# Full products for the first chunk, and the folds of two inputs moved to other quarters

## The chip, the cores and the metric

The kernel runs on one core of a Trainium2 chip. The metric is the time of one execution in microseconds of the device; a profiled execution also leaves a span, from its first to its last instruction. TensorE multiplies matrices and writes PSUM. VectorE, ScalarE and POOL (GpSimd) work on tiles, and SP only issues DMAs. In the profile they are PE (with PEld for its weight loads), DVE, ACT, POOL and SP.

## The reference

```python
batch, seq, dim = (8, 3008, 256)          # x, float32

X = np.fft.fft(x, axis=1)                 # over the sequence
X = np.fft.fft(X, axis=2)                 # over the features
x = X.real

xt = x.transpose(0, 2, 1)
h = np.maximum(xt @ w_tok1, 0.0) @ w_tok2         # 3008 -> 256 -> 3008
u = x + h.transpose(0, 2, 1)
h2 = np.maximum(u @ w_ch1, 0.0) @ w_ch2           # 256 -> 1536 -> 256
return u + h2
```

For each of eight batches this takes the real part of a two-dimensional Fourier transform, mixes along the sequence with a two-layer network, and then along the features with another one.

## The kernel before

All matmuls are in float16 with sums in float32. The work of one batch has three parts.

**The fold.** `fold(b)` (L451) takes the batch's input from `xp` and `xm` and uses the symmetries of the transform: it adds mirrored rows and mirrored columns into `eo`. It is a generator of 12 steps, three for each of four ranges of rows: L463 adds `xm` into `xp` (before the first, L461 and L462 treat column 0), L467 and L472 write the two halves of `eo`. All of them run on VectorE. `load_x(b)` (L157) fills `xp` with four DMAs and `xm` with two gathers, all issued by POOL. There is one buffer of `xp`, of `xm` and of `eo`, so the load of one input waits for the last fold step of the input before it.

**The front.** `front(b)` (L570) and `rest(b)` (L605) form a generator of the transform and the first network: `inner` and `outer` make `z` from `eo`, L596 to L601 make `w`, L613 and L636 the hidden layer `uu`, `third` makes a third of `yt` (L645 on TensorE, L648 on ScalarE, L652 on VectorE), and L730 with L738 make `ut`, the transposed input of the second network, in six chunks of 512 columns (the last has 448). `turn_u(b, c)` turns a chunk back by two DMA transposes on SP, into `rt`, which is needed for the residual.

**The second network.** For each chunk `(b, c)`, `mm1` (L765) makes 12 tiles of the hidden layer `c1` on TensorE (L773), which ScalarE brings out of PSUM with a ReLU (L776). `mm2` (L867) then multiplies with `wc2`. A chunk for which `plain(b, c)` is true takes full products: for each of four row blocks 12 matmuls with 256 columns, and residuals on VectorE. All other chunks take `mm2_sums` (L801), which gets the product of 2 x 2 blocks with seven block products instead of eight. It needs sums of blocks of `c1`, four instructions per half chunk on VectorE (`block_sums`, L790, into `sb` and in place into `c1`), and sums of blocks of `wc2` (`weight_sums`, L235). Its products go to the two PSUM tiles `px` and `py`, all of 128 columns; ScalarE keeps three of them as `m` (L822), VectorE and POOL add them into `osb` (L799), and SP writes `osb` out.

**The order.** It is written out by hand. The loop over `b` and over six chunks `c` has four quarters `s` for each chunk, so a batch has 24 quarters, `sub = 4 * c + s`, from 0. Each quarter issues three of the chunk's `mm1` tiles (six matmuls), and a quarter of `mm2` of the *previous* chunk; between them it takes steps of the generators as lists say:

- `own_plan[b][sub]`: steps of this batch's own front that are left (the `ut` of chunks 1 or 2 to 5);
- `plan[b][sub]`: steps of the next batch's front;
- `early_plan[sub]`: in batch 0, steps of `fold(1)`;
- `fold_plan[b][sub]`: steps of `fold(b + 2)`; in batch 1, of `fold(2)` to its end and then of `fold(3)`.

`load_x(2)` is issued in quarter 11 of batch 0 and `load_x(3)` in quarter 1 of batch 1, `load_x(1)` ahead of the loop. `block_sums` of a chunk run in its quarters 2 and 3 for one half and in the first two quarters of the next chunk for the other half. For chunk (0, 0) all of it runs in the next chunk, as instructions of twice the size. Every engine works off its instructions in the order in which they were issued: a VectorE instruction that waits for data holds all VectorE instructions behind it.

PSUM has three buffers for `pc` ("mm"), three for `pz`, `pw`, `pt`, `pq`, `py` of `third` and `pu` ("f"), and two for the products of `mm2` ("o2").

Of the kernel before, what the change touches and what calls it, by code (L numbers as in the profile page):

```python
# [21 lines left out]
BB = 8  # L22
# [12 lines left out]
NCH = 6  # L35
# [6 lines left out]
def kernel(  # L42
# [42 lines left out]
    def dram(t, offset, ap):  # L85
        return bass.AP(tensor=t, offset=offset, ap=ap)
# [65 lines left out]
    def gather(out_, rows, index):  # L152
        nc.gpsimd.indirect_dma_start(
            out=out_, out_offset=None, in_=rows,
            in_offset=bass.IndirectOffsetOnAxis(ap=index, axis=0))

    def load_x(b):  # L157
        xp = xin.tile([KR, NR, D], FP16, tag="xp", name="xp")
        xm = xin.tile([KG, NR - 1, D], FP16, tag="xm", name="xm")
        for i in range(2):  # L160
            for q, n in ((0, 32), (32, NQ - 32)):
                p0 = i * NQ + q
                nc.gpsimd.dma_start(
                    out=xp[p0:p0 + n, :, :],
                    in_=dram(x_t, (b * S + 16 * i + 64 * q) * D,
                             [[64 * D, n], [1, NR * D]]))
        xmf = xm[:].rearrange("p t d -> p (t d)")
        for k in range(2):
            gather(xmf[:, 8 * D * k:8 * D * (k + 1)], x8, ix8[0:KG, b, k:k + 1])
        return xp, xm  # L170
# [5 lines left out]
    x_tiles = {0: load_x(0)}  # L176
# [50 lines left out]
    HC = NCT // 2  # L227
# [216 lines left out]
    def align_w2(c, th, e):  # L444
        a = slice(8 * c, min(8 * c + 8, NQ))
        copy(e, w2p[:, th, :, a], w2v[:, th, :, a])
# [123 lines left out]
    def front(b):  # L570
        st = state[b]
        if b == 0:
            yield from rest(b)
            return
        eo = st["eo"]
        z = perb.tile([P, 2, 24, 64], FP16, tag="z", name="z")
        for t0 in (11, 6, 1):
            for half in range(2):
                inner(eo, t0, half, z_put(z, half, t0, 0))
                yield  # L580
        for half in range(2):
            def edge(pz, c):
                nc.tensor.matmul(pz[:, 0:24], lhsT=eo[:, 0, c], rhs=t1n[:, half, 0, :],
                                 start=True, stop=not half)
                if half:
                    nc.tensor.matmul(pz[:, 0:24], lhsT=nyq[:], rhs=t1n[:, 0, 0, :],
                                     start=False, stop=True)

            outer(eo, half, z_put(z, half, 0, 0), edge)
            yield  # L590
        w = st["w"] = perb.tile([P, NG, WD], FP16, tag="w", name="w", bufs=2)
        for g in range(NG):
            pw = ps_f("pw")
            za = z[:, 0, 2 * g:2 * g + 2, :].rearrange("p a b -> p (a b)")
            zb = z[:, 1, 2 * g:2 * g + 2, :].rearrange("p a b -> p (a b)")
            nc.tensor.matmul(pw[:, 131:WD], lhsT=zb, rhs=td1[:], start=True, stop=True)  # L596
            nc.tensor.matmul(pw[:, 0:131], lhsT=za, rhs=td0[:], start=True, stop=True)  # L597
            copy(0, w[:, g, 132:WD], pw[:, 132:WD])
            nc.vector.scalar_tensor_tensor(  # L599
                out=w[:, g, 0:131], in0=alt[:], scalar=pw[:, 131:132],  # L600
                in1=pw[:, 0:131], op0=AT.mult, op1=AT.add)  # L601
            yield
        yield from rest(b)
# [153 lines left out]
    CTS = [0, 6, 1, 7, 2, 8, 3, 9, 4, 10, 5, 11]  # L757

    def plain(b, c):
        return (b, c) == (BB - 1, NCH - 1)  # L760

    def tiles(b, c):
        return 1 if c + 1 == NCH and b % 2 == 0 else 2
# [16 lines left out]
    def block_sums(c1, sb, k, which, n):  # L780
        hi = slice(HC + k.start, HC + k.stop)
        lo, up = slice(0, P * n), slice(P * n, 2 * P * n)
        a11, a21 = c1[:, k, lo], c1[:, k, up]
        a12, a22 = c1[:, hi, lo], c1[:, hi, up]
        s0, s1, s2 = (sb[:, i, k, lo] for i in range(3))
        sums = ((s0, a21, a22, AT.add), (s1, s0, a11, AT.subtract),
                (a21, a11, a21, AT.subtract), (s2, a12, s1, AT.subtract))
        for i in which:
            o, x, y, op = sums[i]
            nc.vector.tensor_tensor(out=o, in0=x, in1=y, op=op)  # L790
# [76 lines left out]
    def mm2(b, c, c1, ks, box):  # L867
        if not plain(b, c):
            return mm2_sums(b, c, c1, ks, box)
# [51 lines left out]
    def pair(b, c1):  # L921

        if b % 2 == 0 and b + 1 < BB:
            state["ch"] = work.tile([P, NCT, 64], FP16, tag="ch", name="ch")
            nc.vector.tensor_copy(out=state["ch"][:], in_=c1[:, :, CW - 128:CW - 64])
        elif b % 2:
            nc.vector.tensor_copy(out=c1[:, :, CW - 64:CW], in_=state["ch"][:])


    def take(g, n):  # L930
        for _ in range(n):
            next(g, None)
# [43 lines left out]
    for c in range(2, NCH):  # L976
        for th in range(2):
# [6 lines left out]

    plan = [[0] * 10 + [2] * 10 + [1, 2, 2, 3]] + [[1] * 14 + [2, 1] * 4 + [1, 1]] * (BB - 1)
    own_plan = [[2, 1, 1, 1, 1, 1, 1, 0, 1, 1, 0, 0, 1, 1] + [0] * 10,
                [1, 1, 1, 0, 0, 1, 1, 0, 1, 1, 0, 0, 1, 1] + [0] * 10]
    own_plan += [[1, 1, 1, 0, 0, 1, 1, 0, 1, 1, 0, 0, 1, 1] + [0] * 10] * (BB - 2)
    early_plan = [0] * 5 + [2, 0, 2, 2, 3, 2, 1] + [0] * 12
    fold_plan = [[0] * 8 + [1, 2, 0, 0] * 4 for _ in range(BB)]  # L990
    fold_plan[0] = [0] * 16 + [2, 2, 0, 0, 2, 2, 0, 0]
    fold_plan[1] = [2, 2, 0, 0] + [0] * 4 + [0, 2, 0, 0] + [1, 2, 0, 0] * 2 + [2, 2, 0, 0]
    prev = None
    turned_u = {(0, 0): turn_u(0, 0)}
    for b in range(BB):
        nxt = front(b + 1) if b + 1 < BB else iter(())
        if b != 1:
            folds = fold(b + 2, [nc.vector] * 4) if b + 2 < BB else None
        for c in range(NCH):
            c1 = work.tile([P, NCT, CW], FP16, tag="c1", name="c1", bufs=2)  # L1000
            box = {"rt": turned_u.pop((b, c))}
            if not plain(b, c):
                box["sb"] = work.tile([P, 3, HC, D], FP16, tag="sb", name="sb", bufs=2)
            if c + 1 == NCH and b % 2:
                pair(b, c1)
            for s in range(4):
                sub = 4 * c + s
                n = plan[b][sub]
                mm1(b, c, c1, range(3 * s, 3 * s + 3))
                def now():  # L1010
                    which = 2 * (s % 2), 2 * (s % 2) + 1
                    if s >= 2 and not plain(b, c) and (b or c):
                        block_sums(c1, box["sb"], slice(0, 3), which, tiles(b, c))
                    elif s < 2 and prev is not None:
                        k = slice(3 if b or c > 1 else 0, HC)
                        block_sums(prev[2], pbox["sb"], k, which, tiles(*prev[0:2]))

                if s == 3:
                    now()
                take(own, own_plan[b][sub])  # L1020
                first = 0 if s % 2 else n // 2
                take(nxt, first)
                if s == 0:
                    now()
                if prev is not None:
                    mm2(*prev, s, pbox)
                if s in (1, 2):
                    now()
                take(nxt, n - first)
                if s == 2 and c + 1 < NCH:  # L1030
                    turned_u[b, c + 1] = turn_u(b, c + 1)
                if s == 3 and c + 1 == NCH and b + 1 < BB:
                    turned_u[b + 1, 0] = turn_u(b + 1, 0)
                if b == 0 and sub in (15, 17, 19, 21):
                    align_w2((sub - 15) // 4, (sub - 15) // 2 % 2, 0)
                if b == 0 and sub == 3:
                    weight_sums()
                    for h in range(2):
                        swap_wc1(h)
                if b == 0 and early_plan[sub]:  # L1040
                    take(early, early_plan[sub])
                    if sub == 11:
                        x_tiles[2] = load_x(2)
                if folds is not None and fold_plan[b][sub]:
                    take(folds, fold_plan[b][sub])
                    if b == 1 and sub == 1:
                        x_tiles[3] = load_x(3)
                        folds = fold(3, [nc.vector] * 4)
                if sub == 22 and b and b + 3 < BB:
                    x_tiles[b + 3] = load_x(b + 3)  # L1050
            if c + 1 == NCH and b % 2 == 0:
                pair(b, c1)
            prev, pbox = (b, c, c1), box
        own = nxt
# [32 lines left out]
```

## Time and profile before

| what | value |
|---|---|
| median of 6 runs | 597.96 us (596.6 to 601.55) |
| profiled execution, time | 596.39 us |
| profiled execution, span | 594.6 us |
| TensorE (PE) busy | 581.4 us, 98% |
| VectorE (DVE) busy | 462.3 us, 78% |
| ScalarE (ACT) busy | 439.5 us, 74% |
| POOL busy | 154.0 us, 26% |
| granted TensorE clock | 1.0 |
| start of quarter 4, 5, 6, 7 and 8 of batch 0 (first `mm1` matmul) | 39.89, 42.95, 46.41, 48.81, 51.59 us |
| start of quarter 0 of batch 1 | 102.63 us |

The profile gives, for each engine, the time it was busy; a busy TensorE is not one at its peak, since matmuls overlap and their ends are modelled. A line of the waits reads: who waited, for whom, microseconds in total, times, longest. A line of a timeline reads: start, microseconds, engine, line of the kernel, operation, output<-input, shape, number of instructions, and in brackets the idle time before it with what ended it.

### The profile page before, as it was taken

The page shows a single profiled execution, that of the slowest core. Times are in us where ns is not written, and L with a number is a line of the kernel's source. Part 1 is how long each engine was busy: PE and PEld are TensorE (multiplying, and loading weights), DVE is VectorE, ACT ScalarE, POOL GpSimd, SP SyncE. Part 2 cuts the span into 40 slices and gives each one's busy share as a digit, 9 for nine tenths or more (in the row PEclk, how much of TensorE's full clock was granted, in tenths as well). Part 3 has the DMA queues.
Part 4 walks back from the last instruction along what each step waited for, and adds up shares of the span by engine and source line. Part 5 has one row for each costly group of instructions (what it writes and reads, how often), then busy time and mean ns, then how long its engine had stood idle before and what let it go on. Part 6 is the DMA issues. An engine that isn't in the chain of part 4 may idle for free.

```text
span 594.6 us, 16046 instructions
## 1 busy us (share of the span) xinstructions
PE 581.4 (98%) x6433; PEld 420.1 (71%) x6433; DVE 462.3 (78%) x1079; ACT 439.5 (74%) x997; POOL 154.0 (26%) x253
## 2 busy tenths in 40 slices
PE   5999999999999999999999999999999999999997
PEld 4846667677777677667777667766777777766676
DVE  8879788779796888769788687867888677676573
ACT  7776886877767776786777777788677877767772
POOL 7632412411241121421124111421211121112131
PEclk9999999999999999999999999999999999999999
DMA  8995591782269233754319453493353324233434
GB/s 148 209 189 124 102 139 38 141 137 54 56 115 156 54 67 79 139 87 84 79 38 178 87 75 55 81 178 55 56 70 68 79 56 94 49 72 69 85 56 105
DMA packets 86682, 56.55 MB, mean 95 GB/s; under 512 B 54944, under 2 KB 83552, under 8 KB 85856
## 3 DMA queue, kind: packets, MB, share of 16 engines
q1 hardware_dynamic: 77984, 37.77, 34.4%
q0 software_dynamic: 8320, 17.49, 17.1%
q8 instruction: 50, 0.82, 0.6%
q10 hardware_dynamic: 304, 0.26, 0.2%
q14 instruction: 24, 0.20, 0.1%
HBM read 34.98 MB, written 24.64 MB: 100 GB/s over the span
## 4 chain that ended last, share of the span: by engine, by line
PE 88%; DVE 7%; DMA 2%; issue 1%; ACT 1%; POOL 0%; DVEq 0%; POOLq 0%
PE pc L773 38%; PE px L817 23%; PE py L817 9%; PE pu L730 6%; PE pt L613 4%; DMA xm<-in_x_dram,ix 2%; DVE sb L790 1%; PE pz L518 1%; PE py L645 1%; PE pq L645 1%; PE po L888 1%; PE py L836 1%; PE pw L596 1%; PE pw L597 1%; DVE xp L463 1%
## 5 line engine op out<-in xcount | busy, mean ns | idle before, releaser
L776 ACT ACTIVATE c<-pc 128x512 f16<-128x512 f32 (+1 forms) x574 | 297.4, 594 | 27.1 <-issue 15.2
L799 POOL TENSOR_TENSOR osb<-osb,rt 128x256 f32<-128x256 f32 (+1 forms) x94 | 85.7, 911 | 385.3 <-DVE osb L799 378.2
L817 PEld LDWEIGHTS <-c 128*128 128x128 f16 x2160 | 131.1, 98 | 26.4 <-DVE c L790 0.7
L773 PE MATMUL pc<-ut,wc1p 128*128 128x512 f16 x576 | 140.1, 379 | 0.5 <-DVE ut L305 0.5
L773 PE MATMUL pc<-ut,wc1m 128*128 128x512 f16 (+1 forms) x576 | 134.9, 370 | 0.0
L822 ACT ACTIVATE m<-px 128x256 f32<-128x256 f32 (+1 forms) x141 | 52.7, 374 | 79.5 <-PE px L817 47.6
L817 PEld LDWEIGHTS <-sb 128*128 128x128 f16 x1620 | 96.9, 98 | 11.7 <-issue 0.6
L738 DVE TENSOR_TENSOR ut<-pu,yt 128x512 f16<-128x512 f32 (+1 forms) x94 | 63.1, 672 | 38.9 <-PE pu L730 38.9
L773 PEld LDWEIGHTS <-wc1p 128*128 128x128 f16 x576 | 51.9, 97 | 49.1 <-DMA wc1p<-in_moe_w_ch_dram,ixc 0.8
L773 PEld LDWEIGHTS <-wc1m 128*128 128x128 f16 x576 | 52.9, 98 | 45.0
L817 PE MATMUL px<-wst,c 128*128 128x128 f16 x1080 | 75.8, 219 | 0.5 <-DVE c L790 0.5
L817 PE MATMUL px<-wc,c 128*128 128x128 f16 x1080 | 68.0, 219 | 0.1
L790 DVE TENSOR_TENSOR sb<-sb,c 128x768 f16<-128x768 f16 (+2 forms) x93 | 55.2, 593 | 3.2
L799 DVE TENSOR_TENSOR osb<-py,m 128x256 f32<-128x256 f32 (+1 forms) x94 | 38.2, 406 | 25.0 <-ACT m L822 24.7
L730 PE MATMUL pu<-w2p,uu 128*128 128x512 f16 (+1 forms) x184 | 54.7, 379 | 0.0
L790 DVE TENSOR_TENSOR sb<-c 128x768 f16<-128x768 f16 (+2 forms) x93 | 51.9, 558 | 0.0
L790 DVE TENSOR_TENSOR c<-c 128x768 f16<-128x768 f16 (+2 forms) x93 | 51.3, 552 | 0.0
L790 DVE TENSOR_TENSOR sb<-c,sb 128x768 f16<-128x768 f16 (+2 forms) x93 | 50.8, 546 | 0.0
L307 ACT ACTIVATE z<-pz 128x480 f16<-128x480 f32 (+1 forms) x60 | 39.0, 666 | 5.5 <-PE pz L527 3.0
L599 DVE SCALAR_TENSOR_TENSOR w<-alt,pw 128x131 f16<-128x131 f16 x84 | 29.1, 350 | 15.7 <-ACT w L307 15.3
L652 DVE TENSOR_TENSOR yt<-py,qs 128x512 f16<-128x512 f32 x48 | 30.9, 684 | 10.7 <-ACT qs L648 10.5
L817 PE MATMUL px<-wst,sb 128*128 128x128 f16 x540 | 37.8, 219 | 0.5 <-DVE osb L799 0.5
(201 smaller groups left out, 640.3 us busy)
## 6 DMA issues: line engine op xcount, KB each, us to landing
out_dram<-osb SPq DMA_DIRECT2D x83, 256.0 KB, 3.6
xp<-in_x_dram POOLq DMA_DIRECT2D x16, 272.0 KB
out_dram<-osb SPq DMA_DIRECT2D x11, 192.0 KB, 3.2
xp<-in_x_dram POOLq DMA_DIRECT2D x16, 127.5 KB
rt<-ut SPq DMA_TRANSPOSE x96, 3.8
w2s<-in_moe_w_tok_dram POOLq DMA_DIRECT2D x1, 1504.0 KB
w1p<-in_moe_w_tok_dram POOLq DMA_DIRECT2D x4, 192.0 KB
wc<-in_moe_w_ch_dram POOLq DMA_DIRECT2D x1, 768.0 KB
```

The lines of the kernel that those rows point to most:

```text
L307: nc.scalar.activation(out=out_, in_=in_, func=AFT.Copy)
L599: nc.vector.scalar_tensor_tensor(out=w[:, g, 0:131], in0=alt[:], scalar=pw[:, 131:132], in1=pw[:, 0:131], op0=AT.mult, op1=AT.add)
L613: nc.tensor.matmul(pt[:, o:o + n], lhsT=hw[:, g, th * P:th * P + P], rhs=w[:, g, f:f + n], start=(g == 0), stop=(g == NG - 1))
L652: nc.vector.tensor_tensor(out=yt[:, h, CW * c:CW * c + CW], in0=py[:], in1=qs[:], op=op)
L730: nc.tensor.matmul(pu[:, 0:n], lhsT=uu[:, th, int(minus), h, :], rhs=w2_cols(b, c)[:, th], start=(th == 0), stop=(th == 1))
L738: nc.vector.tensor_tensor(out=ut[:, h, 0:n].rearrange("p (a b) -> p a b", b=64), in0=pu[:, 0:n].rearrange("p (b a) -> p a b", b=64), in1=y ...
L773: nc.tensor.matmul(pc[:, 0:n], lhsT=wc[:, h, ct * P:(ct + 1) * P], rhs=ut[:, h, 0:n], start=(h == 0), stop=(h == 1))
L776: nc.scalar.activation(out=c1[:, ct, 0:n], in_=pc[:, 0:n], func=AFT.Relu)
L790: nc.vector.tensor_tensor(out=o, in0=x, in1=y, op=op)
L799: eng.tensor_tensor(out=o, in0=x, in1=y, op=AT.add)
L817: nc.tensor.matmul(o[:, t], lhsT=a(k)[:, f:f + P], rhs=w(k), start=(first and t == 0 and k == 0), stop=(k == HC - 1), skip_group_check=True)
L822: nc.scalar.activation(out=m[:, i, t1], in_=pa[:, 0], func=AFT.Copy)
```

## The change

Chunk (0, 0) becomes a `plain` one, with full products, and has no block sums any more. The steps of `fold(1)` begin in quarter 4 instead of 5. The steps of `fold(2)` leave quarters 16 and 17 of batch 0: six are taken in quarters 20 and 21, three each, and six in quarters 0 and 1 of batch 1, three each. `load_x(2)` is issued in quarter 10 of batch 0 instead of 11, `load_x(3)` in quarter 2 of batch 1 instead of 1. In batch 1 three of the own steps go from quarters 0, 1 and 2 to 1, 2 and 4. The rest of the diff writes the same conditions in another form.

```diff
--- before.py
+++ after.py
@@ -757,7 +757,7 @@
     CTS = [0, 6, 1, 7, 2, 8, 3, 9, 4, 10, 5, 11]
 
     def plain(b, c):
-        return (b, c) == (BB - 1, NCH - 1)
+        return (b, c) in ((0, 0), (BB - 1, NCH - 1))
 
     def tiles(b, c):
         return 1 if c + 1 == NCH and b % 2 == 0 else 2
@@ -984,12 +984,13 @@
 
     plan = [[0] * 10 + [2] * 10 + [1, 2, 2, 3]] + [[1] * 14 + [2, 1] * 4 + [1, 1]] * (BB - 1)
     own_plan = [[2, 1, 1, 1, 1, 1, 1, 0, 1, 1, 0, 0, 1, 1] + [0] * 10,
-                [1, 1, 1, 0, 0, 1, 1, 0, 1, 1, 0, 0, 1, 1] + [0] * 10]
+                [0, 1, 1, 0, 1, 1, 1, 0, 1, 1, 0, 0, 1, 1] + [0] * 10]
     own_plan += [[1, 1, 1, 0, 0, 1, 1, 0, 1, 1, 0, 0, 1, 1] + [0] * 10] * (BB - 2)
-    early_plan = [0] * 5 + [2, 0, 2, 2, 3, 2, 1] + [0] * 12
+    early_plan = [0] * 4 + [2, 2, 1, 2, 1, 2, 2] + [0] * 13
     fold_plan = [[0] * 8 + [1, 2, 0, 0] * 4 for _ in range(BB)]
-    fold_plan[0] = [0] * 16 + [2, 2, 0, 0, 2, 2, 0, 0]
-    fold_plan[1] = [2, 2, 0, 0] + [0] * 4 + [0, 2, 0, 0] + [1, 2, 0, 0] * 2 + [2, 2, 0, 0]
+    fold_plan[0] = [0] * 20 + [3, 3, 0, 0]
+    fold_plan[1] = [3, 3] + [0] * 7 + [2] + [0, 0, 1, 2, 0, 0, 1, 2, 0, 0, 2, 2, 0, 0]
+    load_at = [10, 2]
     prev = None
     turned_u = {(0, 0): turn_u(0, 0)}
     for b in range(BB):
@@ -1009,11 +1010,11 @@
                 mm1(b, c, c1, range(3 * s, 3 * s + 3))
                 def now():
                     which = 2 * (s % 2), 2 * (s % 2) + 1
-                    if s >= 2 and not plain(b, c) and (b or c):
+                    if s >= 2 and not plain(b, c):
                         block_sums(c1, box["sb"], slice(0, 3), which, tiles(b, c))
-                    elif s < 2 and prev is not None:
-                        k = slice(3 if b or c > 1 else 0, HC)
-                        block_sums(prev[2], pbox["sb"], k, which, tiles(*prev[0:2]))
+                    elif s < 2 and prev is not None and not plain(*prev[0:2]):
+                        block_sums(prev[2], pbox["sb"], slice(3, HC), which,
+                                   tiles(*prev[0:2]))
 
                 if s == 3:
                     now()
@@ -1037,16 +1038,15 @@
                     weight_sums()
                     for h in range(2):
                         swap_wc1(h)
-                if b == 0 and early_plan[sub]:
+                if b == 0:
                     take(early, early_plan[sub])
-                    if sub == 11:
-                        x_tiles[2] = load_x(2)
-                if folds is not None and fold_plan[b][sub]:
+                if folds is not None:
                     take(folds, fold_plan[b][sub])
-                    if b == 1 and sub == 1:
-                        x_tiles[3] = load_x(3)
+                if b < 2 and sub == load_at[b]:
+                    x_tiles[b + 2] = load_x(b + 2)
+                    if b:
                         folds = fold(3, [nc.vector] * 4)
-                if sub == 22 and b and b + 3 < BB:
+                if b and sub == 22 and b + 3 < BB:
                     x_tiles[b + 3] = load_x(b + 3)
             if c + 1 == NCH and b % 2 == 0:
                 pair(b, c1)
```

## The prediction

> **What bounds the kernel now.** I read the busy shares first, then the waits of TensorE, then the timelines of TensorE and VectorE (the "quarters" below are numbered from 0 and begin with the mm1 group of six 128x512 matmuls).
>
> ```profile
> PE 581.4 (98%) x6433; PEld 420.1 (71%) x6433; DVE 462.3 (78%) x1079; ACT 439.5 (74%) x997; POOL 154.0 (26%) x253
> ```
>
> TensorE is the bound: a change pays only if it removes TensorE work or a wait of TensorE. Its waits from 41 to 103 us:
>
> ```profile
> PE px L817 <- DVE c L790: 0.5, 1, 0.5
> PE px L817 <- DVE osb L799: 0.5, 2, 0.2
> PE pw L596 <- ACT z L307: 0.2, 1, 0.2
> ```
>
> The same question for 126 to 594 us has no line at all. So what can be won by order alone lies before 126 us. The waits printed there are short because ends of matmuls are modelled; the starts say more. TensorE's timeline (start, duration):
>
> ```profile
> 44.68 0.83 PE L817 MATMUL py<-wst,sb 128*128 128x128 f16 x12
> 45.74 0.83 PE L817 MATMUL px<-wst,sb 128*128 128x128 f16 x12 [0.23 <-DVE osb L799]
> 46.41 1.46 PE L773 MATMUL pc<-ut,wc1p 128*128 128x512 f16 x6
> ...
> 56.38 0.85 PE L817 MATMUL py<-wst,sb 128*128 128x128 f16 x12
> 57.48 0.83 PE L817 MATMUL px<-wst,sb 128*128 128x128 f16 x12 [0.25 <-DVE osb L799]
> ```
>
> Twelve 128-column matmuls take 0.67 from start to start where nothing holds them (45.74 to 46.41). From 44.68 to 45.74 they took 1.06, so 0.39 was lost; before 57.48 about 0.41 in the same way. Read so, further losses are 0.15 at 50.92, 0.17 at 65.72, 0.34 at 72.13, 0.65 at 83.85, 0.30 at 88.98 and 0.15 at 104.30. VectorE's timeline shows what is late:
>
> ```profile
> 43.41 0.95 DVE L790 TENSOR_TENSOR sb<-c 128x1536 f16<-128x1536 f16 x1
> 44.40 0.96 DVE L790 TENSOR_TENSOR sb<-sb,c 128x1536 f16<-128x1536 f16 x1
> 45.27 0.42 DVE L799 TENSOR_TENSOR osb<-px,m 128x256 f32<-128x256 f32 x1
> 45.61 0.68 DVE L738 TENSOR_TENSOR ut<-pu,yt 128x512 f16<-128x512 f32 x1
> 46.20 1.44 DVE L790 TENSOR_TENSOR c<-c 128x1536 f16<-128x1536 f16 x1
> 47.57 0.95 DVE L790 TENSOR_TENSOR sb<-c,sb 128x1536 f16<-128x1536 f16 x1
> ...
> 53.78 1.65 DVE L463 TENSOR_TENSOR xp<-xp,xm 94x1020 f16<-94x1020 f16 x1
> ...
> 81.81 0.23 DVE L461 TENSOR_TENSOR xp<-xp,xm 94x16 f16<-94x16 f16 x1 [1.15 <-DMA xm<-in_x_dram,ix]
> ```
>
> The residual of the first chunk sits behind two block sums and frees px only at 45.7. Four such sums are 4.30 us. At 53.78 a fold piece of x1 takes 1.65 where the same shape takes 0.68 elsewhere, and the residual that frees px comes at 57.01. At 81.81 the fold of x2 heads VectorE's queue before its second gather has landed; c<-c (83.25) comes behind it, and TensorE stands at 83.85.
>
> **The change part by part.**
>
> *Full products for chunk (0,0).* Removed: 84 matmuls of 128 columns, at 1.34/24 = 0.0558 each: 4.69. Added: 48 of 256 columns; twelve of that shape (L836) take 1.31 from 107.47 to 108.78, so 5.24. TensorE works 0.55 longer. The losses at 45.74 and 50.92, 0.54, belong to the removed products and their sums and go. Net +0.01: from 41.62 to the start of quarter 8 stays at 9.97. VectorE loses four sums (4.30); four 0.42 residuals stay four, now with rt read backwards in two of them (nearest row, osb<-px,rt: 0.42; bounds 0.4 to 0.7, so at most 1.2 in all, inside the 4.30). ScalarE loses three keeps of 0.38, POOL two adds (0.67 and 1.21). None of these is on the path by itself. SP's queue keeps its order: the transposes of turn_u stay in their quarters, and the chunk's two output DMAs still follow quarter 7. weight_sums stays in quarter 3, now first needed in quarter 9.
>
> Here a rule stands against a row. The Trainium skill, "TensorE: Matmul & The Clock Gate", Back-to-back issue gap, gives about 81 ns per 128-column matmul in streams that load weights each time, and calls N/2.4 + 2.5 an isolated figure. With it the removed products would cost 84 x 0.081 = 6.80 (an estimate) and this part would win 1.56. This trace loads weights before each matmul and still shows 55.8 ns, at a granted clock of 1.00; the row decides.
>
> *Fold of x1 from quarter 4 on, not 5.* The same 12 steps, 2-2-1-2-1-2-2 instead of 2-0-2-2-3-2-1 from quarter 5. By quarter 8 seven steps are done instead of four, with 4.30 us less beside them. So the lateness of VectorE at 57.48 (0.41) and 65.72 (0.17; px waited for the residual at 65.25) goes: -0.58. It also reaches xm sooner. VectorE would come to L461 at about 43.4, while packets of the load queue end between 44.0 and 45.0: VectorE waits about 1.1. Behind that wait stand the ut of quarter 5 (needed in quarter 12), and the residuals of quarter 5, which also need rt (landed at 46.0, when POOL's rt copy starts). I cost it at nothing: with data at 44.5 two steps take 1.44, ut 0.6, residuals 0.7, so the first po is free near 47.3, while TensorE asks for that bank at 51.6 (quarter 8). Without that cover each us is one lost.
>
> *load_x(2) at quarter 10, not 11.* Four xp issues (2.12) and two gathers (0.97, 0.94) on POOL, now earlier because the fold ends earlier. Queued behind are the add of quarter 11 and later rt copies, none waited for by TensorE within 5 us. x2 should land at 76 to 80, before quarter 20.
>
> *Fold of x2 from quarter 20, not 16.* The wait at 81.81 and the pieces behind it leave quarters 16 to 19, and with them 0.65 (83.85) and 0.30 (88.98; px waited for the residual at 88.51): -0.95.
>
> *What comes back.* Quarters 20 and 21 take three steps each, and quarters 0 and 1 of batch 1 too. VectorE idles 0.43 and 1.61 at 92.3 and 96.0, which covers the extra 1.1 of quarter 20; the extra 0.33 of quarter 21 leaves about 0.15 before py asks at 100.46. In batch 1 third(2) (8 matmuls 0.45, yt 1.29) leaves quarter 0 for 1, and ut of chunk 2 moves to 2 and 4, still ahead of turn_u in 6. The 0.15 at 104.30 goes with it. Quarter 0 of VectorE gets lighter by about 1.1, quarter 1 heavier by 1.3. Counting along the queue the residual osb<-py,m of quarter 2, 1.05 ahead of its user before (112.19 to 113.24), is about 0.2 ahead, and px of chunk (1,0) about level. Bounds: 0 (all absorbed) to 1.7 (every step hit). POOL adds decide: the 1.65 fold piece above ran under POOL's add from 53.67 to 54.88. The Trainium skill, "SBUF — State Buffer", Who interferes with whom, says that a VectorE instruction with two SBUF inputs and a GpSimd one that reads SBUF block each other for a whole instruction; this speaks against three pieces in quarters in which POOL adds (107.71, 0.48: fold piece 0.91 instead of 0.68). By the rule each hit costs up to a whole add, 1.2; by the row nearest in place 0.23. I take 0.45.
>
> load_x(3) goes a quarter later: before it was issued at 111.69 to 116.4 and L461 ran at 132.41 without a wait; 2.5 later stays hidden.
>
> Sum: +0.01 - 0.58 - 0.95 - 0.15 + 0.45 = **-1.2 us**. The profiled execution (span 594.6, 596.39 in all) would become 593.4; the median shown is 597.96, 1.6 above that execution, so 596.8.
>
> **The rivals.**
> 1. *The crowd takes it all back.* Two or three fold pieces in batch 1, quarters 0 to 2, run under POOL adds, VectorE is 1.7 behind and osb and sb are waited for. For: margins of 0.2. Against: third(2) was moved out of the fullest quarter. Time 598.0; it would take more than 1.7 to be slower.
> 2. *Slower: x1 is met before it has landed.* At quarter 4 VectorE stands before L461. TensorE is untouched while the data land by about 48.6 (44.5 plus the 4.1 of slack above); each us later is a us lost, and beyond 50.3 the whole is slower. Landing at 53.5, as if the load took 9 us more, gives 4.9 - 1.7 = +3.2: 601.2. For: before, that load had 4 us in hand, now none. Against: it lands at 44.5 here and shares its queue with nothing later.
> 3. *More goes than counted.* If late VectorE also made the 0.34 at 72.13 and nothing comes back, -2.0: 596.0. If the 1.6 between the profiled execution and the median comes from the same late gathers, part of it goes too: down to 595.0.
> 4. *It does not do what it says:* quarters 5 to 8 stay late since rt, not the sums, holds VectorE. Then -0.4: 597.6.
>
> **How the numbers follow.** Forecast 0.5; rival 1 0.17, rival 2 0.06, rival 3 0.17, rival 4 0.1. A measurement of this kernel tells about 0.5% (3 us) from no change. The six runs spread from 596.6 to 601.55, which moves a median by 1 to 2 either way, so the range is 594.2 to 599.6. Faster by over 0.5%, below 595.0: most of rival 3's second half and the low tail, 0.18. Slower, above 600.9: rival 2 and the high tail, 0.08. Within: 0.74.
>
> **What would show it.** Right: 48 po rows of 256 columns from 41.6 on, no L790 row of 1536; mm1 of quarter 8 near 51.6; L461 of x1 waiting about 1 us at 43 to 45 with no TensorE wait behind; no wait at 57.5 and 83.9; L461 of x2 near 92 without one. Wrong: waits of TensorE for osb or sb between 100 and 118 of over 1 us; L461 waiting past 48; any wait after 126 us.

## The result, and the profile after

The changed kernel takes 594.24 us (median of 29 runs, 594.17 to 595.71). The kernel before takes 597.38 (66 runs, 595.25 to 601.55). The ratio is 0.9944, 95% interval 0.9933 to 0.9955: faster by about 0.5%, 3.1 us between the medians. The prediction was 596.8. Note the spreads: 6.3 us before, 1.5 after, and 27 of the 29 later runs within 0.8.

The busy shares of the changed kernel, from its page:

```profile
PE 580.8 (98%) x6397; PEld 419.7 (71%) x6397; DVE 458.4 (77%) x1075; ACT 438.0 (74%) x994; POOL 152.4 (26%) x251
```

TensorE remains the bound. Its list of waits from 36 us to the end is now empty. TensorE's timeline at the place that lost 0.41 before (start, duration):

```profile
57.59 0.83 PE L817 MATMUL py<-wst,sb 128*128 128x128 f16 x12
58.26 0.83 PE L817 MATMUL px<-wst,sb 128*128 128x128 f16 x12
58.93 1.46 PE L773 MATMUL pc<-ut,wc1p 128*128 128x512 f16 x6
```

Both groups of twelve take 0.67 from start to start; nothing is lost. VectorE's timeline at the first fold instruction of x1 and of x2:

```profile
46.44 0.23 DVE L461 TENSOR_TENSOR xp<-xp,xm 94x16 f16<-94x16 f16 x1 [1.75 <-DMA xm<-in_x_dram,ix]
...
92.01 0.22 DVE L461 TENSOR_TENSOR xp<-xp,xm 94x16 f16<-94x16 f16 x1
```

The fold of x1 now waits 1.75 us for its data, and no TensorE wait follows; the fold of x2 no longer waits. One more line has to be read before the two profiles are compared. This wait of TensorE lies in the setup, which the change does not touch:

```profile
PE ph L432 <- DMA w1m<-in_moe_w_tok_dram: 1.2, 1, 1.2
```

It makes this profiled execution, at 595.59, one of the slowest of the changed kernel: quarter 0 starts at 33.53 instead of 32.34. From the first matmul of quarter 0 to the end of the span it is 593.8 - 33.53 = 560.27, against 594.6 - 32.34 = 562.26 before: 1.99 less. The medians differ by 3.14, so 1.15 is not in this pair of profiles. The experiments look for it.

### The profile page after: what moved, and what is told of

The parts are those of the page before. It is cut to its first block, busy times and chain, and to the rows that moved or that the text cites. A ratio compares the mean times of both kernels' runs of the same rounds, so it can differ in the third digit from the quotient of the medians.

```text
span 593.8 us, 15959 instructions
## 1 busy us (share of the span) xinstructions
PE 580.8 (98%) x6397; PEld 419.7 (71%) x6397; DVE 458.4 (77%) x1075; ACT 438.0 (74%) x994; POOL 152.4 (26%) x251
## 4 chain that ended last, share of the span: by engine, by line
PE 95%; DMA 3%; DVE 1%; issue 0%; POOL 0%; POOLq 0%; DVEq 0%
PE pc L773 41%; PE px L817 25%; PE py L817 10%; PE pu L730 7%; PE pt L613 4%; PE po L888 2%; PE pz L518 2%; DMA w1m<-in_moe_w_tok_dram 2%; DMA xm<-in_x_dram,ix 1%; PE pq L645 1%; PE py L645 1%; PE py L836 1%; PE pw L596 1%; PE pw L597 1%; PE ph L432 0%; PE ph L430 0%
## 5 line engine op out<-in xcount | busy, mean ns | idle before, releaser
L799 POOL TENSOR_TENSOR osb<-osb,rt 128x256 f32<-128x256 f32 (+1 forms) x92 | 84.1, 914 | 373.1 <-DVE osb L799 365.9
L817 PEld LDWEIGHTS <-c 128*128 128x128 f16 x2112 | 128.1, 98 | 24.8
L817 PEld LDWEIGHTS <-sb 128*128 128x128 f16 x1584 | 94.6, 98 | 10.4
L817 PE MATMUL px<-wst,c 128*128 128x128 f16 x1056 | 74.0, 219 | 0.0
L817 PE MATMUL px<-wc,c 128*128 128x128 f16 x1056 | 66.5, 219 | 0.0
L790 DVE TENSOR_TENSOR sb<-sb,c 128x768 f16<-128x768 f16 (+1 forms) x92 | 54.2, 589 | 3.2
L790 DVE TENSOR_TENSOR c<-c 128x768 f16<-128x768 f16 (+1 forms) x92 | 50.9, 553 | 0.0
L790 DVE TENSOR_TENSOR sb<-c 128x768 f16<-128x768 f16 (+1 forms) x92 | 50.5, 549 | 0.0
L790 DVE TENSOR_TENSOR sb<-c,sb 128x768 f16<-128x768 f16 (+1 forms) x92 | 49.8, 542 | 0.0
L817 PE MATMUL py<-wst,sb 128*128 128x128 f16 x528 | 37.1, 219 | 0.0
```

The costliest lines, as they stand in the source:

```text
L799: eng.tensor_tensor(out=o, in0=x, in1=y, op=AT.add)
L817: nc.tensor.matmul(o[:, t], lhsT=a(k)[:, f:f + P], rhs=w(k), start=(first and t == 0 and k == 0), stop=(k == HC - 1), skip_group_check=True)
```

## The experiments

Theory A: the second gather of x2 lands at a different time in each run; the fold of x2 stands at the head of VectorE's queue from quarter 16 on, and the wait passes to TensorE. Theory B: the gain and the spread come from VectorE's lateness by the sums of chunk (0,0) and the fold of x1. Theory C: the spread comes from the setup. "Before" stands for 597.38, the median of its 66 runs; "beside" stands for the 23 to 35 further runs of it that belong to an experiment, with medians of 596.6 to 597.1. The ratios are on record against these; they need not equal the quotient of two medians. Since the two medians differ by up to 0.8, a gain is given against both where it matters. Where a time of landing is given, it is the end of the last 4,096-byte packet of the gathers, 0.3 to 0.4 us before the end of the DMA in a chain.

**before_again.** No edit; the kernel before in another profiled execution.

> The kernel before, profiled once more, unchanged. Theory A (the second gather of x2 lands at different times, and VectorE stands before it at quarter 16): if the profiled time is well above 596.4, the extra time is found at L461 of x2, VectorE waits there for more than 1.15 us and TensorE loses about as much at 83 to 86 us as the time is longer. Theory B (the extra time is VectorE being late by the sums of chunk (0,0) and the fold of x1): the extra is between 43 and 66 us, at px or py waiting for osb. Theory C (it is the setup): quarter 0 begins later than 32.3.

It took 598.71, 2.3 more than the first profiled execution. Its chain, VectorE's and TensorE's timelines:

```profile
70.69 13.31 DMA xm<-in_x_dram,ix
```
```profile
84.12 0.23 DVE L461 TENSOR_TENSOR xp<-xp,xm 94x16 f16<-94x16 f16 x1 [3.84 <-DMA xm<-in_x_dram,ix]
```
```profile
86.16 0.68 PE L817 MATMUL px<-wst,c 128*128 128x128 f16 x9 [3.14 <-DVE c L790]
```

The gather was done 13.31 us after its issue instead of 10.62, VectorE stood 3.84 instead of 1.15, and TensorE 3.14 instead of 0.48. The 2.7 more that TensorE waits cover the 2.3 of the time. Quarter 0 began at 32.23, so it is not the setup. Theory A.

**fold2_only.** The kernel before with the fold of x2 (and batch 1's own steps) moved alone.

```diff
-    fold_plan[0] = [0] * 16 + [2, 2, 0, 0, 2, 2, 0, 0]
+    fold_plan[0] = [0] * 20 + [3, 3, 0, 0]
     (fold_plan[1] and own_plan[1] as in the change)
```

> Only the fold of x2 is moved (quarters 20 and 21 and 0 and 1 of batch 1, with the own steps of batch 1); load_x(2) stays at quarter 11, sums and fold of x1 as before. Theory A: the median falls by 2.0 to 2.8 us and the runs lie within 1.5 us of each other as those of the changed kernel do. Theory B or C: it falls by at most 1.0 and the spread of some 6 us stays.

594.88 (594.67 to 595.34), ratio 0.9949, interval 0.9925 to 0.9972: 2.5 below before and 1.9 below the runs beside it (596.77), so most of the 3.1 us, and the spread is gone. x2 was issued as late as before (last gather at 70.79); L461 ran at 91.36 without a wait.

**plain_only.** The kernel before with full products alone.

```diff
-        return (b, c) == (BB - 1, NCH - 1)
+        return (b, c) in ((0, 0), (BB - 1, NCH - 1))
```

> Only chunk (0,0) is changed to full products; both folds and loads as before. Theory A: -0.3 to -1.0 us (VectorE has 4.3 us less in front of the fold of x1, so load_x(2) comes a little sooner), spread mostly as before. Theory B: -1.5 us or more, and the spread shrinks. The prediction's own sum for this part alone is about 0 on TensorE's path.

595.70 (595.08 to 596.81), ratio 0.9966 (0.9943 to 0.9988): 1.1 below the runs beside it, 1.7 below before, and a smaller spread. That is more than was expected of A, and against before it is what was expected of B, so this run does not part the two. Its trace has both. The last gather was issued 0.9 earlier than in the first profile of before, at 70.14, x2 landed at 80.00, and VectorE waited 0.44 at L461: by starts TensorE loses 0.13 at 83 us instead of 0.88. And up to 66 us it no longer loses the 1.13 of before, for which full products add 0.55 of work.

**load2_later.** The kernel before with load_x(2) one quarter later.

```diff
-                    if sub == 11:
+                if b == 0 and sub == 12:
                         x_tiles[2] = load_x(2)
```

> The kernel before with load_x(2) issued one quarter later (12 instead of 11), nothing else. Theory A: each microsecond of later landing is one on TensorE's path: +2 to +3.5 us, and the profile shows VectorE waiting 3 to 5 us at L461 of x2. Theory B or C: within 0.5 us of before.

606.08 (603.77 to 608.8), ratio 1.0132 (1.0090 to 1.0174): 9.3 above the runs beside it, about three times what was expected. The issue was only 2.0 later than in before_again. Chain, VectorE and TensorE:

```profile
72.72 16.42 DMA xm<-in_x_dram,ix
```
```profile
89.25 0.23 DVE L461 TENSOR_TENSOR xp<-xp,xm 94x16 f16<-94x16 f16 x1 [9.33 <-DMA xm<-in_x_dram,ix]
```
```profile
91.29 1.14 PE L817 MATMUL px<-wst,c 128*128 128x128 f16 x9 [8.62 <-DVE c L790]
...
92.44 2.63 PE L773 MATMUL pc<-ut,wc1m 128*128 128x512 f16 x6
```

The direction is A's. But the transfer itself also took longer when it started later, 16.42 us after 13.31, which A did not contain; no_out below says why. After the wait TensorE also ran at a lower clock for a while (last section).

**no_plain.** The changed kernel without full products (the kernel before with the lists of the change and load_x(2) at quarter 10; load_x(3) stays at quarter 1).

```diff
-        return (b, c) in ((0, 0), (BB - 1, NCH - 1))
+        return (b, c) == (BB - 1, NCH - 1)
```

> The changed kernel without full products: chunk (0,0) keeps seven block products and its four sums; folds, loads and own steps as in the changed kernel (594.24 us). The prediction's sum says that full products cost 0.55 of TensorE and save 0.54 of waiting, so within 0.3 of the changed kernel if nothing else hangs on them. Rival: the 4.3 us of sums that VectorE must do beside the earlier fold of x1 make px and py wait at 45 to 66 us, +0.5 to +1.5 us.

595.81 (595.73 to 597.97): +1.57 over the changed kernel, the rival's case. Its waits of TensorE from 33 to 120 us:

```profile
PE px L817 <- DVE c L790: 0.8, 1, 0.8
PE px L817 <- DVE osb L799: 0.5, 2, 0.2
```

By starts TensorE loses 0.39 before 45.64, 0.93 before 48.96, 0.09 before 51.70, 0.26 before 54.35 and 0.49 before 58.58, 2.16 in all; less the 0.55 that block products save, 1.61. Two fold steps at 45.5 to 47.4 stand ahead of the sum c<-c that px waits for. The run is also 0.93 above fold2_only, from which it differs by the earlier fold of x1 and the earlier load alone: beside the block sums, the earlier fold of x1 costs time.

**fold1_back.** The changed kernel with the fold of x1 as before.

```diff
-    early_plan = [0] * 4 + [2, 2, 1, 2, 1, 2, 2] + [0] * 13
+    early_plan = [0] * 5 + [2, 0, 2, 2, 3, 2, 1] + [0] * 12
-    load_at = [10, 2]
+    load_at = [11, 2]
```

> The changed kernel with the fold of x1 from quarter 5 on again and load_x(2) at quarter 11. Theory A (what counts is that x2 has landed when it is folded, and it is folded at quarter 20 here): within 0.4 us of 594.24, no spread, no wait at L461 of x2. Theory that the earlier fold of x1 makes the gain (lateness at 57 and 66 us goes): +0.5 us or more.

594.23 (594.17 to 595.70). The earlier fold of x1 and the earlier load of x2 are worth nothing beside the other parts.

**fold2_back.** The changed kernel with the fold of x2 as before.

```diff
-    fold_plan[0] = [0] * 20 + [3, 3, 0, 0]
+    fold_plan[0] = [0] * 16 + [2, 2, 0, 0, 2, 2, 0, 0]
     (fold_plan[1], own_plan[1] as before; load_at = [10, 1])
```

> The changed kernel with the fold of x2 from quarter 16 on again (load_x(2) stays at quarter 10, full products and early fold of x1 stay). Theory A: the earlier load lands near 77 us and quarter 16 reaches L461 at 79 to 80, so the wait is gone in most runs; 594.2 to 595, some runs above. If only the later fold helps: 595.5 to 597 with the spread of before.

594.70 (594.61 to 596.03), no wait at L461 of x2 (79.97). So an early load cures the wait as well as a late fold does, and 0.46 remains for places in VectorE's queue: by starts TensorE loses 0.09 at 83.22 and 0.29 at 87.61, behind the fold, and 0.16 at 102.94, where batch 1's own steps are back too.

**load2_at14.** The changed kernel with load_x(2) at quarter 14.

```diff
-    load_at = [10, 2]
+    load_at = [14, 2]
```

> The changed kernel with load_x(2) at quarter 14 instead of 10. The issue would run at about 73 to 78 us and the second gather land 10 to 16 us after the last issue, at 88 to 94; L461 comes at 92. Theory A: 0 to +3 us, with a spread and a wait at L461 as in the kernel before. If the time of landing does not matter: within 0.2 of 594.24.

594.21 (594.16 to 595.53). The issue moved less than I thought (last gather at 71.81 instead of 68.56; with the load at quarter 10 POOL had stood 7.07 us before it, until the last fold step of x1 freed the buffers). But x2 landed at 87.82 instead of 76.05, and L461 still ran at 90.63 without a wait. With the fold at quarter 20 the time of landing is free over some ten microseconds. It does not test a landing after 91.

**own_back.** The changed kernel with batch 1's own steps as before.

```diff
-                [0, 1, 1, 0, 1, 1, 1, 0, 1, 1, 0, 0, 1, 1] + [0] * 10]
+                [1, 1, 1, 0, 0, 1, 1, 0, 1, 1, 0, 0, 1, 1] + [0] * 10]
```

> The changed kernel with the own steps of batch 1 in quarters 0, 1, 2 again instead of 1, 2, 4, so that VectorE has third(2) beside three fold steps in quarter 0. The prediction's term for the crowd (+0.45 with a bound of 1.7): +0.3 to +1.5 us over 594.24, with TensorE waiting for osb, yt or ut at 103 to 116 us. Rival (VectorE had room there): within 0.2 of 594.24.

594.97 (594.94 to 595.54), +0.73. TensorE's timeline shows the waits for VectorE in batch 1:

```profile
102.43 0.38 PE L645 MATMUL py<-tp,w 128*128 128x128 f16 x4 [0.19 <-DVE ut L738]
...
113.70 1.50 PE L817 MATMUL px<-wc,c 128*128 128x128 f16 x24 [0.19 <-DVE osb L799]
```

They print as 0.38 of the 0.73, since ends of matmuls are modelled; by starts each of the two places loses 0.35. The crowd is real; moving three own steps is what avoids it.

**fold1_only.** The kernel before with the new `early_plan` and load_x(2) at quarter 10.

> The kernel before with only the fold of x1 from quarter 4 on and load_x(2) at quarter 10; sums of chunk (0,0) and the fold of x2 at quarter 16 stay. As fold2_back and no_plain suggest: early stalls as in no_plain (about 1.3 more than before at 48 to 58 us), the load of x2 issued some 2 us sooner; 595.8 to 597.2 us with less spread than before. The prediction's own sum for this step alone would be -0.6 us of lateness at 57 and 66.

596.31 (596.22 to 597.65). TensorE's waits are those of no_plain, 0.8 and 0.5; L461 of x2 ran at 81.34 without a wait, and the spread is small. 596.31 is 0.50 above no_plain, as fold2_back is 0.46 above the changed kernel: the places of the fold of x2 and of batch 1's own steps, twice.

**turn_late.** The kernel before with one pair of transposes a quarter later.

```diff
-                if s == 2 and c + 1 < NCH:
+                if s == (3 if (b, c) == (0, 3) else 2) and c + 1 < NCH:
                     turned_u[b, c + 1] = turn_u(b, c + 1)
```

> The kernel before with one pair of transposes, that of rt of chunk (0,4), issued in quarter 15 instead of 14, so that it is queued on SP behind less time of the load of x2. If the transposes that run among the gather's packets hold one DMA engine back and make the gather's tail late: less spread and -0.5 to -2 us. If they do not matter: median and spread as before.

595.19 (595.04 to 595.58), ratio 0.9978 (0.9962 to 0.9994): 2.2 below before, 1.4 below the runs beside it (596.58), and a spread of 0.5, with nothing moved on VectorE, POOL or TensorE. In before_again SP issues the pair beside the load:

```profile
68.59 6.85 SPq L753 DMA_TRANSPOSE rt<-ut  x2
```

Here SP's timeline and VectorE's are:

```profile
67.05 13.22 SPq L858 DMA_DIRECT2D out_dram<-osb  x4
80.32 5.43 SPq L753 DMA_TRANSPOSE rt<-ut  x4
```
```profile
80.14 0.71 DVE L461 TENSOR_TENSOR xp<-xp,xm 94x16 f16<-94x16 f16 x1
```

No transpose runs beside the load (POOL issued it at 66.97 to 71.6); x2 landed at 78.76, and L461 did not wait for it.

**no_out.** The kernel before without the output DMAs of chunks (0,1) and (0,2).

```diff
-        if s == 3:
+        if s == 3 and (b, c) not in ((0, 1), (0, 2)):
             for i in range(2):
```

> The kernel before without the output DMAs of chunks (0,1) and (0,2) (these rows of the output are not written), which SP issues at about 67 and 79 us. If SP's output beside the load of x2 makes it land late: x2 lands by 79 us, -1.5 to -2.5 us and a small spread. If not: median and spread as before.

600.08 (598.09 to 601.34), ratio 1.0063 (1.0040 to 1.0087): 3.5 above the runs beside it, slower with less to move, against both expectations. Its SP timeline, and VectorE's:

```profile
67.06 3.60 SPq L753 DMA_TRANSPOSE rt<-ut  x2
```
```profile
83.80 0.23 DVE L461 TENSOR_TENSOR xp<-xp,xm 94x16 f16<-94x16 f16 x1 [3.57 <-DMA xm<-in_x_dram,ix]
```

Without an output ahead of them SP issues the transposes at 67.06, just as POOL begins to issue the load (66.97). The DMA queues from 74 to 79 us (packets, MB, share of 16 engines; q0 is POOL's load, q1 SP's), first turn_late, then no_out:

```profile
q0 software_dynamic: 259, 0.88, 88.2%
...
q1 hardware_dynamic: 17, 0.01, 1.0%
```
```profile
q0 software_dynamic: 132, 0.47, 91.0%
q1 hardware_dynamic: 394, 0.10, 31.2%
```

Beside 0.10 MB of transposes, five microseconds bring 0.47 MB of the load instead of 0.88, in the same share of packet time. In the trace's packet records the 4,096-byte packets of the gather take 0.32 us at the median in both kernels, but some are held up: none takes more than 0.32 in turn_late, while in no_out 15 of 192 take over 1 us, up to 3.55.

All 14 profiles agree. The transposes make packets of 256 bytes, 1,024 for a pair. Counted here are those that start between the first packet of the load of x2 and its landing, beside the time from the issue of the last gather to the landing:

| profiles | 256-byte packets beside the load | from the last issue to the landing |
|---|---|---|
| after, own_back, fold2_back, turn_late | 0 | 7.5 to 8.1 us |
| fold1_only, no_plain | 102, 393 | 8.0, 8.3 us |
| fold1_back, fold2_only, plain_only, before | 456 to 657 | 9.9 to 10.4 us |
| before_again, no_out | 1,003, 1,024 | 13.0, 12.7 us |
| load2_at14, load2_later | 1,378, 1,487 | 16.0 us each |

A slow load also meets more packets, so the table alone would not give the cause; turn_late and no_out, in which the transposes move and the issue of the load does not, do. The table also answers load2_later: its load runs on into the next pair of transposes, issued at 79.25.

So theory A holds, and its source is found: transposes queued on SP beside the load of x2. How they hold it up is not resolved in full. In before_again only one gather packet takes over 1 us; but from 79 us to the landing at 83.71 the load has just 13 of these packets left, about three a microsecond, most of them at 0.32. That is the pace of one DMA engine of 16 with a backlog, an inference, since the records do not name the engine. Nor is it known why the same program meets the transposes at different points from run to run.

No version tried is clear of the changed kernel: fold1_back and load2_at14 are level with it (594.23, 594.21), with no wait of TensorE printed after quarter 0.

## Why the prediction was right or wrong

**Right.** *Full products in TensorE's time*: predicted +0.01 on the 9.97 from the first products of chunk (0,0) to quarter 8; measured 42.81 to 52.80, 9.99. The row of 55.8 ns decided rightly against the 81 of the Trainium skill ("TensorE: Matmul & The Clock Gate", Back-to-back issue gap): with it, as an estimate, this stretch would have come out 1.56 shorter. *The wait for x1*: predicted 1.1 and hidden; it was 1.75 and hidden; L461 ran at 46.44, of which 1.2 is the later setup. *x2*: landing between 76 and 80 (76.05), L461 near 92 (92.01).

**Wrong: the term for the wait at L461 of x2.** The step that failed is the -0.95 for the fold of x2, together with the 1.6 that was added to come from the profiled execution to a median. The -0.95 priced the wait by one execution, 0.65 at 83.85 and 0.30 at 88.98, and that execution was one of the better ones: in before_again the first place alone cost TensorE 3.3 by starts. The 1.6 was carried over as if the change left it alone, when most of it went with this wait: in turn_late, where the wait is cured, the profiled execution (595.20) stands at the median (595.19). The run fold2_only, without the wait and with the fold in its new place, is 1.9 to 2.5 below before; the spread of 596.6 to 601.55, put down as what a measurement cannot tell, went with it. A hint was on the page: a gather that lands at 81.7 and is needed at 80.7 has no margin, so its run-to-run scatter goes one to one into the time. Rival 3 named it and gave it 595.0, 3.0 below its 597.96 and close to the 3.1 measured, with too small a chance. The predicted chances, 0.74 for no change that can be told, follow from that.

One loss in the same place was not read at all: nine matmuls of 0.0558 from 83.85 on make 84.35, but the next one starts at 84.58. This 0.23 goes too.

**Wrong credit: the fold of x1.** 0.58 was booked for it (the lateness at 57 and 66 us). The run fold1_back shows 0.0; no_plain beside fold2_only shows that without full products it costs 0.9. That 0.58 belongs to full products, which take 4.3 us of sums off VectorE: in plain_only the places at 57 and 66 us are already free of loss. So the -0.58 came true for a reason other than the one given.

**Wrong size: the crowd.** +0.45 was booked and 0.07 came back (at 111.99). The fear was fold pieces held by POOL's adds. All four L463 pieces of x2, at 92.38, 97.06, 105.36 and 109.21, took 0.68, the undisturbed time; one POOL add, at 105.58, met the fold and cost the next piece 0.11 (L467, 0.54 instead of 0.43), less than the 0.23 and the 1.2 that the prediction weighed. The run own_back shows what the crowd costs if the own steps stay where they were, 0.73; the moved steps avoid it.

**The sum.** On the pair of profiles, from quarter 0 on: -1.2 predicted, -1.99 measured. The missing 0.79 is the crowd's 0.45, 0.21 at 72.13 (0.34 lost before, 0.13 after) and 0.23 at 84.58, less some 0.1 that TensorE still loses at 88.24 and 111.99. Rival 3's -2.0 for the same pair is in part luck: it counted all of the 0.34 and not the 0.23. The other 1.15 between the medians goes with x2's wait beyond the first profiled execution: fold2_only and turn_late, which each cure that wait, take the spread away. By parts, from medians and in this order: the fold of x2 with the own steps 2.5 (597.38 to 594.88; 1.9 against the runs beside it), full products with load_x(3) 0.65 (to 594.23), the fold of x1 nothing. Another order gives other parts, since plain_only, by an earlier load, also cures some of the wait.

## What to carry to other kernels

When identical runs differ by more than the change can bring, look for a wait on a transfer that lands at the very moment when it is needed, and price that wait over runs and not from one profile. An instruction that may wait for data belongs where an in-order engine has nothing urgent behind it: the fold four quarters later, the load some 2 us earlier, or one pair of transposes a quarter later each cured the same wait here. Credit a stall to a part only after undoing that part alone.

## What the runs showed of the hardware

DMA transposes slow a load beside them far beyond their bytes: here a pair moves 0.26 MB in 256-byte packets, and the load of 1.6 MB landed 12.7 to 13.0 us after its last issue with some 1,000 of them beside it, 7.5 to 8.1 with none (table above). And a long wait of TensorE costs more than its length. load2_later in stretches of 4 us after its wait of 8.62 (PE, PEld, DVE, ACT, POOL busy, granted clock, DMA share, GB/s):

```profile
88.00:92.00 4.00, 0.71 (x7) 0.72 (x8) 2.68 (x8) 0.00 (x0) 0.00 (x0) 0.50 0.23 43
92.00:96.00 4.00, 4.00 (x33) 2.44 (x31) 3.97 (x11) 2.34 (x5) 0.00 (x0) 0.65 0.00 0
96.00:100.00 4.00, 4.00 (x61) 3.45 (x59) 3.39 (x8) 2.65 (x7) 2.17 (x3) 1.00 0.15 30
```

The mean granted clock was 0.50, then 0.65, and 1.00 after 96 us; the six matmuls at 92.44 took until 94.91, 2.47 instead of 1.30. After the wait of 3.14 in before_again six such matmuls took 1.30 (87.00 on, in the timeline), so a wait of that length did not pay this. It may be part of the tail of before: of its 88 runs beside the experiments, 22 list a mean clock of 0.997 or 0.994, all of them of 598.4 us or more, and of the other 66 only two are that long; no run of the changed kernel lists less than 0.998. These runs have no trace, so that their clock fell after the wait for x2 is not shown.
